# A chunked linear attention with a feed-forward layer: the decays of the first 128 tokens spread over rows on TensorE instead of through DRAM, and a new order

## The chip, the cores and the metric

One core of a Trainium2 chip runs the kernel. The time is device microseconds of one execution; lower is better. Matrix products run on TensorE (PE, its weight loads PEld), elementwise work on VectorE (DVE), ScalarE (ACT) and GpSimd (POOL); SyncE (SP) only issues DMAs, as ScalarE does too.

## What is computed

Four batches of 8 heads, 768 tokens, head size 32, state size 16. The attention is a recurrence cut into pieces: within a piece a product of C and B is weighted by ratios of decays and multiplied with x, and a state is carried on. Then each token (256 wide, all heads side by side) goes through a normalization and two weight matrices, with its input added at the end.

```python
def _attn_ref(x, a, B, C):
    log_a = np.log(np.clip(a, 1e-06, 1.0))
    ...
        cum = np.cumsum(la, axis=-1)
        L = np.exp(cum[:, :, :, None] - cum[:, :, None, :]) * causal
        M = np.einsum('bhin,bhjn->bhij', Cc, Bc) * L
        y[:, :, sl] = np.einsum('bhij,bhjd->bhid', M, xc) + y_inter
...
def _moe_ref(x, g_ln, w_ch1, w_ch2):
    xn = (x - mu) / np.sqrt(var + 1e-06) * g_ln
    ch = np.maximum(xn @ w_ch1, 0.0) @ w_ch2
    return (x + ch).astype(np.float32)
```

## The kernel before

The tokens go in six blocks t = 0 to 5 of 128 tokens of all batches and heads; u = 0, 1 is the half of the batches. Every instruction is written out by hand, in one table of steps (`ISSUE`): a step is a name and its block, half or part, and after a colon the engine (v VectorE, p GpSimd, a ScalarE, s SyncE's queue). Each engine runs its steps in the order of the table, and an instruction that waits holds up all behind it on its engine. A DMA is a step too: it waits on the engine whose queue issues it, and each also waits until the DMA eight places before it in the whole program has landed, since eight semaphores are used in turn.

Steps of the start: `ld:s a` loads the decays with one row for each batch part and head (128 rows of 192), `clip`, `u` and `d` (lines 289 to 298) scan them into products since and until the borders of 32 tokens, `uds`. These stand on 128 rows of 6 x 32, but C and B stand on rows of (head, state) with 512 columns of (batch, token), so each head's decays are wanted on 16 rows. `ro` (line 301) writes `uds` to a DRAM tile `scr`, and `ld ud` (line 134) reads it back with a broadcast over the 16 rows. `C` (line 305) multiplies C by it into `cs`, `B` (line 319) B into `bs`, and `cm` parts `cs` into even and odd heads. `G` (line 345) is the product of the two, `R` (line 351) weights it with `WW`. `WW` is a causal mask (`ones`) overwritten by ratios of decays (`W`), which come from logarithms (`l2` to `l4`), products (`e`) and exponentials (`x`). `V` (line 376) multiplies R by x, `Z` the state's increment (from `be`, B with its decay), `I` adds what the state gives, `y` copies the sum out of PSUM, `yh` and `yl` split it in an upper and a lower part, `T` turns it to tokens and `tc` copies that.

The two weight matrices come as 64-bit integers (`ld w1`, `ld w2`, 512 KB each part) and are turned to floats by `k0` and `kr` (ScalarE, lines 182 and 201), `k1` to `k3` (VectorE) and `f` (GpSimd, line 206); w1 is centred by two float32 products `wc` on TensorE (lines 217, 218); `wh` and `wl` split the result. `h` (line 457) is the first layer for 128 of 1024 hidden columns, in block 0 for each half u by itself, `hh` and `hl` its ReLU split in two; `o` (line 477) is the second layer for one batch, `oe` its end and `od` its store. `fill` is a product of zeros that nothing reads.

PSUM has two pools, one of five banks for the attention and one of three for the rest. `ud`, `c`, `b`, `bt` and `xt` tiles have two buffers each.

Of the kernel before, what the change touches and what calls it, by code (L numbers as in the profile page):

```python
# [50 lines left out]
def shape_constants():  # L51

    k = np.arange(P)
    sub = k // SUB
# [19 lines left out]
def linear_attention_ffn(ctx, tc, xv, a, bt, bn, cn, w1, w2, consts, out):  # L74
    nc = tc.nc
# [33 lines left out]
    scr = dr.tile([2, NT, P, SUB], F32, name="scr")  # L109
# [11 lines left out]
    def load(what, *at, e=nc.sync):  # L121
# [5 lines left out]
        elif what == "ud":  # L127
# [5 lines left out]
            rows = scr[i, t].rearrange("(h c) k -> h (c k)", h=NH)  # L133
# [166 lines left out]
    def spread_out(i, e=nc.sync):  # L300
        e.dma_start(scr[i].rearrange("t r k -> r t k"), uds[:, i].rearrange("p (t k) -> p t k", k=SUB))
# [184 lines left out]
    def fill(i, bank):  # L486
# [106 lines left out]
```

## Time and profile before

| | us |
|---|---|
| median of 3 runs | 211.73 |
| lowest, highest | 209.41, 485.84 |
| the profiled execution | 210.03 |
| its span, first to last instruction | 208.2 |
| TensorE busy in it | 199.8 (96%) |
| VectorE, ScalarE, GpSimd busy | 122.8, 83.1, 54.8 |

The span is what the trace shows; 1.83 us of the execution lie around it. A busy TensorE is not a TensorE at its peak: a product that waits in its pipeline counts as busy.

### The profile page before, as it was taken

The page shows a single profiled execution, that of the slowest core. Times are in us where ns is not written, and L with a number is a line of the kernel's source. Part 1 is how long each engine was busy: PE and PEld are TensorE (multiplying, and loading weights), DVE is VectorE, ACT ScalarE, POOL GpSimd, SP SyncE. Part 2 cuts the span into 40 slices and gives each one's busy share as a digit, 9 for nine tenths or more (in the row PEclk, how much of TensorE's full clock was granted, in tenths as well). Part 3 has the DMA queues.
Part 4 walks back from the last instruction along what each step waited for, and adds up shares of the span by engine and source line. Part 5 has one row for each costly group of instructions (what it writes and reads, how often), then busy time and mean ns, then how long its engine had stood idle before and what let it go on. Part 6 is the DMA issues. An engine that isn't in the chain of part 4 may idle for free.

```text
span 208.2 us, 4661 instructions
## 1 busy us (share of the span) xinstructions
PE 199.8 (96%) x1956; PEld 172.2 (83%) x1956; DVE 122.8 (59%) x258; ACT 83.1 (40%) x170; POOL 54.8 (26%) x57
## 2 busy tenths in 40 slices
PE   8959998999999999999999999999999999999994
PEld 8956466899899876799978899878899889998993
DVE  4847859899958699831657561557443444335310
ACT  3748449889171372431024760143401261123200
POOL 0024533668688065160001821040020000000000
PEclk9996699999999999999999999999999999999999
DMA  6799996073134030012262101010000200001011
GB/s 217 222 296 408 279 254 211 20 238 118 55 127 130 25 122 6 3 17 87 66 212 79 54 0 52 2 50 0 5 3 7 94 0 28 25 0 52 3 50 50
DMA packets 11573, 19.08 MB, mean 92 GB/s; under 512 B 2592, under 2 KB 6048, under 8 KB 11552
## 3 DMA queue, kind: packets, MB, share of 16 engines
q1 hardware_dynamic: 8792, 14.00, 20.9%
q10 hardware_dynamic: 2760, 4.79, 6.9%
q8 instruction: 15, 0.25, 0.5%
q14 instruction: 6, 0.05, 0.1%
HBM read 15.44 MB, written 3.34 MB: 90 GB/s over the span
## 4 chain that ended last, share of the span: by engine, by line
PE 74%; DMA 16%; DVE 5%; issue 2%; SPq 1%; ACT 1%; DVEq 0%
PE po L477 32%; PE ph L457 28%; DMA raw<-in_w_dram 8%; PE G L345 5%; DMA ud<-scr 5%; PE yps L376 4%; PE yt L425 2%; PE yps L364 2%; DMA scr<-uds 2%; DMA a<-in_a_dram 1%; DVE WW L158 1%; DVE hl L469 1%; SPq L134 1%; PE Z L385 1%; DVE R L351 1%
## 5 line engine op out<-in xcount | busy, mean ns | idle before, releaser
L477 PE MATMUL po<-w,hh 128*128 128x256 f32 x384 | 68.7, 281 | 0.0
L477 PEld LDWEIGHTS po<-w,hh 128*128 128x128 f32 x384 | 59.0, 188 | 1.9 <-issue 0.9
L463 ACT ACTIVATE hh<-ph 128x512 fp32r<-128x512 f32 (+1 forms) x56 | 29.7, 541 | 73.7 <-PE ph L457 53.9
L457 PE MATMUL ph<-yh,w 128*128 128x512 f32 (+1 forms) x224 | 55.3, 369 | 1.0 <-DVE hl L469 0.7
L477 PE MATMUL po<-w,hl 128*128 128x256 f32 x192 | 53.6, 279 | 0.0
L469 DVE SCALAR_TENSOR_TENSOR hl<-ph,hh 128x512 fp32r<-128x512 f32 (+1 forms) x56 | 33.7, 607 | 22.8 <-ACT hh L463 22.7
L457 PEld LDWEIGHTS ph<-yh,w 128*128 128x128 f32 x224 | 37.4, 188 | 9.4 <-DVE hl L469 1.8
L351 DVE TENSOR_TENSOR R<-G,WW 128x512 f32<-128x512 f32 x48 | 30.9, 677 | 9.9 <-PE G L345 8.9
L477 PEld LDWEIGHTS po<-w,hl 128*128 128x128 f32 x192 | 36.1, 188 | 0.0
L481 DVE SCALAR_TENSOR_TENSOR o<-po,rstd,ytok 128x256 f32<-128x256 f32 x24 | 11.6, 482 | 34.6 <-PE po L477 34.6
L457 PE MATMUL ph<-yl,w 128*128 128x512 f32 (+1 forms) x112 | 31.3, 360 | 0.5 <-DVE yl L418 0.5
L457 PEld LDWEIGHTS ph<-yl,w 128*128 128x128 f32 x112 | 20.0, 189 | 4.0 <-DVE yl L418 0.7
L345 PE MATMUL G<-cm,bs 32*128 32x256 f32 x192 | 17.3, 421 | 2.6 <-DVE cm L315 2.3
L418 POOL TENSOR_TENSOR yl<-y,yh 128x512 fp32r<-128x512 f32 x8 | 10.2, 1285 | 34.3 <-ACT yh L158 19.7
L345 PEld LDWEIGHTS G<-cm,bs 32*128 32x128 f32 x192 | 10.9, 192 | 6.3 <-issue 3.9
L158 ACT COPY WW<-wt 32x512 f32<-32x512 f32 (+2 forms) x27 | 14.8, 611 | 2.8 <-DVE R L351 2.8
L206 POOL TENSOR_TENSOR top<-top,raw 128x512 int32<-128x512 int32 x8 | 12.0, 1509 | 10.3 <-DVE top L196 4.1
L305 POOL TENSOR_TENSOR cs<-c,ud 128x512 f32<-128x512 f32 x5 | 6.6, 1324 | 26.5 <-DVE c L323 23.4
L376 PE MATMUL yps<-R,xt 128*32 128x128 f32 x384 | 12.1, 274 | 0.0
L376 PEld LDWEIGHTS yps<-R,xt 128*32 128x32 f32 x384 | 10.1, 110 | 1.6 <-DVE top L187 0.8
L490 PE MATMUL idle<-const-float32-0.0 128*128 128x128 f32 x62 | 10.3, 343 | 0.8 <-PEq L581 0.8
L490 PEld LDWEIGHTS idle<-const-float32-0.0 128*128 128x128 f32 x62 | 10.0, 257 | 0.7 <-issue 0.7
(83 smaller groups left out, 179.7 us busy)
## 6 DMA issues: line engine op xcount, KB each, us to landing
out_dram<-o SPq DMA_DIRECT2D x24, 128.0 KB, 1.7
raw<-in_w_dram SPq DMA_DIRECT2D x5, 512.0 KB, 7.4
xt<-in_x_dram SPq DMA_DIRECT2D x5, 512.0 KB, 6.7
ud<-scr SPq DMA_DIRECT2D x7, 256.0 KB
raw<-in_w_dram ACTq DMA_DIRECT2D x3, 512.0 KB, 8.3
b<-in_bn_dram SPq DMA_DIRECT2D x5, 256.0 KB
ud<-scr ACTq DMA_DIRECT2D x5, 256.0 KB
c<-in_cn_dram SPq DMA_DIRECT2D x4, 256.0 KB, 10.0
```

Of the source, the lines that this page charges most:

```text
L158: (e.copy if e is nc.scalar else e.tensor_copy)(dst, src)
L206: e.tensor_tensor(out=f, in0=f, in1=words.pop((w, *at))[0], op=ALU.add)
L345: nc.tensor.matmul(G[q][:, v], bs[r, tok], cm[r, :, tok], start=True, stop=True)
L351: nc.vector.tensor_tensor(out=R.rearrange("p v i k -> p v (i k)"), in0=tiles.pop(("G", t, u, q)).rearrange("p v i k -> p v (i k)"), in1=WW ...
L376: nc.tensor.matmul(tiles["y", t, u, g][32 * k:32 * k + 32, v], x[:, b * NH + h], tiles["R", t, u, h // 2][:, v, h % 2], start=(t == 0), st ...
L418: e.tensor_tensor(out=tiles["yl", t][:, :, tok], in0=tiles["y32", t][:, :, tok], in1=tiles["yh", t][:, :, tok].bitcast(F32), op=ALU.subtract)
L457: nc.tensor.matmul(ph, W1[m // 4, k][:, s, mc], v[:, k, tok], start=(i == 0), stop=(i == len(cmb) - 1))
L463: nc.scalar.activation(tiles["hh", t, m][:, tok], tiles["ph", t, m, u], AF.Relu)
L469: nc.vector.scalar_tensor_tensor(out=tiles["hl", t, m][:, tok], in0=tiles.pop(("ph", t, m, u)), scalar=0.0, in1=tiles["hh", t, m][:, tok]. ...
L477: nc.tensor.matmul(po, tiles[v, t, m][:, cols], W2[m // 2,][:, s, (m % 2) * DM:(m % 2 + 1) * DM], start=(n == 0), stop=(n == len(cmb) - 1))
L481: nc.vector.scalar_tensor_tensor(out=o, in0=tiles.pop(("po", t, b)), scalar=tiles["rstd", t][:, b], in1=tiles["ytok", t][:, b], op0=ALU.mu ...
L490: nc.tensor.matmul(ps.tile([P, P], F32, tag=bank, name=f"idle{i}"), zero.to_broadcast([P, P]), zero.to_broadcast([P, P]), start=True, stop ...
```

## The change

The scan products of block 0 no longer go through `scr`, which now holds five blocks. `U` multiplies the block's 32 columns, repeated 16 times, with a 0/1 matrix that keeps on each row only its own place, and `ur` multiplies the result by a second 0/1 matrix, which sums over rows; the sum of one number and zeros stands in a PSUM bank, in the place of the `ud` tile of block 0. The two matrices make the first load of constants 144 columns wider.

```diff
+C_ROW = C_SUM + 8
+C_COL = C_ROW + P
+C_CAUSAL = C_COL + P // NH
...
+    c[:, C_ROW:C_COL] = (k // DS)[:, None] == (k // DS)[None, :]
+    c[:, C_COL:C_CAUSAL] = (k % (P // NH))[:, None] == np.arange(P // NH)
...
-    scr = dr.tile([2, NT, P, SUB], F32, name="scr")
+    scr = dr.tile([2, NT - 1, P, SUB], F32, name="scr")
...
-            rows = scr[i, t].rearrange("(h c) k -> h (c k)", h=NH)
+            rows = scr[i, t - 1].rearrange("(h c) k -> h (c k)", h=NH)
...
-        e.dma_start(scr[i].rearrange("t r k -> r t k"), uds[:, i].rearrange("p (t k) -> p t k", k=SUB))
+        e.dma_start(scr[i].rearrange("t r k -> r t k"), uds[:, i, SUB:].rearrange("p (t k) -> p t k", k=SUB))
+
+    def own_columns(i, e=nc.vector):
+        m = tiles["m", i] = hp.tile([P, P // NH, SUB], F32, tag="hl", name=f"own{i}")
+        e.tensor_tensor(out=m, in0=uds[:, i, :SUB].unsqueeze(1).to_broadcast([P, P // NH, SUB]), in1=cst[:, C_COL:C_CAUSAL].unsqueeze(2).to_broadcast([P, P // NH, SUB]), op=ALU.mult)
+
+    def all_rows(i):
+        ps = tiles["ud"[i], 0] = ps_att.tile([P, TB], F32, tag="att", name=f"rows{i}")
+        nc.tensor.matmul(ps, cst[:, C_ROW:C_COL], tiles.pop(("m", i)).rearrange("p j k -> p (j k)"), start=True, stop=True)
...
-ld:s a, inv:v, ld:a early, az:p, ini:v, ld:a w1 0 1, clip, ld:a w1 0 0, cf, u, ro:a 0, iv, d, l1, ones:v 0, l2, l3, ro:s 1, l4, k0 1 0 1, fill 0 att,
+ld:s a, ini:v, az:p, clip, inv:v, u, ld:a early, ld:a c 0, iv, ld:s w1 0 0, U:v 0, cf, d, l1, U:v 1, fill 0 att, fill 1 att, fill 2 att, fill 3 att,
```

Of the DMAs, ScalarE's queue keeps the constants and c of block 0; all others are issued by SyncE. There are 25 fills instead of 31. The rest of the table is in another order, with some steps on other engines: over the whole program VectorE gets 17 more instructions (three more `W` copies, three more `yl`, two `U` among them, and three `be` fewer), GpSimd eleven fewer.

VectorE at the start, where block 0's `cs` and `bs` are made; before:

```order
L289 TENSOR_SCALAR AZ<-a_104 128x6x31
L292 SCALAR_TENSOR_TENSOR uds<-AZ,ini 128x192
L295 RECIPROCAL inv<-uds 128x6
L298 SCALAR_TENSOR_TENSOR uds<-AZ,inv 128x192
L244 TENSOR_SCALAR cst<-cst 128x192
L158 COPY WW_91<-cst 128x2048
L253 TENSOR_TENSOR ll<-cst,lh 128x192
L158 COPY WW_92<-cst 128x2048
```

And now, to the same place and on to `bs`:

```order
L299 RECIPROCAL inv<-uds 128x6
L310 TENSOR_TENSOR own_119<-uds,cst 128x512
L302 SCALAR_TENSOR_TENSOR uds<-AZ,inv 128x192
L248 TENSOR_SCALAR cst<-cst 128x192
L310 TENSOR_TENSOR own_124<-uds,cst 128x512
L162 COPY WW_91<-cst 128x2048
L319 TENSOR_TENSOR cs_173<-c_114,rows_160 128x512
L257 TENSOR_TENSOR ll<-cst,lh 128x192
L191 TENSOR_SCALAR top_175<-top_175 128x512
L191 TENSOR_SCALAR top_187<-top_187 128x512
L333 TENSOR_TENSOR bs_201<-b_168,rows_170 128x512
```

The two `own` products come in between the scans, one of the two mask copies (`WW_92`) has gone to ScalarE, and `cs` and `bs` read PSUM (`rows`) and stand ahead of most of the first weights' work (`top`).

ScalarE in the middle of the start, from the first centred weights to the copies of y; before:

```order
L158 CAST w_328<-wc_309 128x512
L182 ACTIVATE top_342<-raw_230 128x512
L182 ACTIVATE top_344<-raw_306 128x512
L152 DMA raw_385<-in_w_dram 128x1024
L158 CAST w_389<-wc_323 128x512
L201 ACTIVATE raw_230<-raw_230 128x512
L158 COPY y_393<-yps_347 128x256
L158 COPY y_393<-yps_367 128x256
```

And now:

```order
L205 ACTIVATE raw_237<-raw_237 128x512
L287 COPY em<-emps 128x96
L288 COPY emt<-emps 128x24
L162 CAST w_319<-wc_308 128x512
L186 ACTIVATE top_324<-raw_279 128x512
L162 CAST w_326<-wc_321 128x512
L186 ACTIVATE top_334<-raw_212 128x512
L162 COPY y_403<-yps_359 128x256
```

The issue of a load of w2 (`raw_385`, part 3) between the casts is gone from ScalarE; `top_324` is the first work on part 0 of w2 (`raw_279`), which SyncE now loads.

SyncE's first loads; before:

```order
L126 DMA a_104<-in_a_dram 128x192
L301 DMA scr<-uds 128x6x32
L142 DMA c_179<-in_cn_dram 128x512
L142 DMA b_194<-in_bn_dram 128x512
L134 DMA ud_203<-scr 128x1x512 x2
L155 DMA cst<-in_consts_dram 128x326
L147 DMA raw_211<-in_w_dram 128x1024
```

And now:

```order
L130 DMA a_104<-in_a_dram 128x192
L151 DMA raw_117<-in_w_dram 128x1024
L151 DMA raw_162<-in_w_dram 128x1024
L146 DMA bt_165<-in_bt_dram 128x512
L146 DMA b_168<-in_bn_dram 128x512
L159 DMA cst<-in_consts_dram 128x326
L151 DMA raw_209<-in_w_dram 128x1024
L156 DMA raw_212<-in_w_dram 128x1024
L151 DMA raw_237<-in_w_dram 128x1024
L146 DMA c_239<-in_cn_dram 128x512
L146 DMA xt_261<-in_x_dram 128x1024
L305 DMA scr<-uds 128x5x32
```

The first two parts of w1 (`raw_117`, `raw_162`) come from SyncE now, and `scr` is written after x of block 0 is issued; part 0 of w2 is the next row.

## Rows read from the trace of the kernel before

**Rows 1.** The top of the page: busy us of each engine, its share of the span of 208.2 us, instructions.

```profile
PE 199.8 (96%) x1956; PEld 172.2 (83%) x1956; DVE 122.8 (59%) x258; ACT 83.1 (40%) x170; POOL 54.8 (26%) x57
```

**Rows 2.** The chain of work that ended last, in order of time: start us, us, what; from 16 us on, and of TensorE's dense part a few pieces of each kind.

```profile
26.26 11.28 DMA raw<-in_w_dram
...
39.55 3.15 PE ph L457 x24
...
51.80 1.08 PE G L345 x16
...
56.91 1.88 PE yps L376 x64
58.80 0.45 PE Z L385 x32
...
84.00 0.44 PE yt L425 x4
...
87.18 1.03 PE yps L364 x32
...
121.37 5.61 PE po L477 x48
...
187.12 6.83 PE ph L457 x30
...
205.19 0.48 DVE o L481
```

**Rows 3.** Instructions in order of time, from 0 to 17 us: start us, us, engine, line, what, count, and in brackets the engine's idle time before it and what ended it.

```profile
0.76 7.43 PE L490 MATMUL idle<-const-float32-0.0 128*128 128x128 f32 x38 [0.76 <-PEq L581]
3.81 0.62 ACT L241 CAST cfr<-cst 128x512 fp32r<-128x512 uint8 x1 [1.81 <-DMA cst<-in_consts_dram]
5.14 1.22 DVE L158 COPY WW<-cst 128x2048 f32<-128x2048 f32 x1
10.03 1.64 ACT L158 COPY WW<-wt 32x512 f32<-32x512 f32 x3
11.48 0.69 DVE L305 TENSOR_TENSOR cs<-c,ud 128x512 f32<-128x512 f32 x1 [1.54 <-DMA ud<-scr]
14.89 1.15 PE L345 MATMUL G<-cm,bs 32*128 32x256 f32 x16 [2.33 <-DVE cm L315]
16.15 1.89 DVE L351 TENSOR_TENSOR R<-G,WW 128x512 f32<-128x512 f32 x3 [0.62 <-PE G L345]
```

**Rows 4.** The same view from 20 to 52 us.

```profile
20.09 2.08 PE L217 MATMUL wc<-top,gd 128*128 128x512 f32 x2
28.30 0.35 ACTq L152 DMA_DIRECT2D raw<-in_w_dram  x1
28.69 0.59 ACT L158 CAST w<-wc 128x512 fp32r<-128x512 f32 x1 [3.00 <-DMA xt<-in_x_dram]
28.95 1.02 PE L218 MATMUL wc<-top,gneg 128*128 128x512 f32 x2
31.47 1.76 DVE L418 TENSOR_TENSOR yl<-y,yh 128x512 fp32r<-128x512 f32 x2 [0.54 <-ACT yh L158]
33.29 0.51 PE L457 MATMUL ph<-yl,w 128*128 128x256 f32 x2 [0.54 <-DVE yl L418]
48.84 0.40 PE L477 MATMUL po<-w,hh 128*128 128x256 f32 x2
```

**Rows 5.** Groups of instructions with their shapes kept apart: line, engine, operation, shapes, count, busy us, mean ns of one, idle us before them.

```profile
L158 ACT COPY y<-yps 128x256 f32<-128x256 f32 x16 | 5.6, 378 | 4.1 <-PE yps L376 3.9
L313 ACT ACTIVATE cm<-cs,cst 128x512 f32<-128x512 f32 x6 | 4.4, 734 | 3.3 <-POOL cs L305 2.8 <-DVE cs L305 0.5
L351 DVE TENSOR_TENSOR R<-G,WW 128x512 f32<-128x512 f32 x48 | 30.9, 677 | 9.9 <-PE G L345 8.9 <-ACT WW L158 1.1
L196 DVE SCALAR_TENSOR_TENSOR top<-raw,top 128x512 int32<-128x512 int32 x8 | 5.3, 681 | 0.0
L191 DVE TENSOR_SCALAR top<-top 128x512 int32<-128x512 int32 x8 | 3.3, 437 | 0.0
L315 POOL TENSOR_SCALAR cm<-cs,cst 128x512 f32<-128x512 f32 x3 | 4.9, 1625 | 0.1
```

**Rows 6.** VectorE's `be` beside a GpSimd instruction and the same operation with GpSimd idle, from the instructions in order of time.

```profile
54.82 1.57 POOL L315 TENSOR_SCALAR cm<-cs,cst 128x512 f32<-128x512 f32 x1
55.08 0.98 DVE L329 TENSOR_TENSOR be<-bt,pend 128x512 f32<-128x512 f32 x1
...
72.08 0.66 DVE L329 TENSOR_TENSOR be<-bt,pend 128x512 f32<-128x512 f32 x1
```

**Rows 7.** Stretches of the span: us, then busy us (instructions) of each engine, TensorE's granted clock, share of the DMA engines, GB/s moved.

```profile
0.00:5.00 5.00, 4.24 (x20) 4.28 (x21) 1.98 (x8) 1.90 (x2) 0.33 (x6) 1.00 0.63 212
5.00:10.00 5.00, 4.92 (x43) 4.73 (x43) 4.79 (x10) 3.53 (x9) 0.00 (x0) 1.00 0.80 227
10.00:15.00 5.00, 2.67 (x27) 2.50 (x27) 2.04 (x5) 2.93 (x7) 0.50 (x2) 1.00 0.86 273
15.00:20.00 5.00, 4.75 (x34) 3.25 (x34) 3.86 (x9) 3.64 (x10) 2.95 (x2) 0.72 1.03 409
20.00:25.00 5.00, 5.00 (x8) 2.23 (x8) 4.18 (x7) 2.61 (x5) 2.86 (x2) 0.60 1.05 308
...
8.00:12.00 4.00, 3.92 (x43) 3.73 (x42) 2.46 (x6) 3.23 (x8) 0.00 (x0) 1.00 0.58 182
```

More of the change, by code (lines that the diff above doesn't have):

```diff
@@ L494, in linear_attention_ffn @@
         ld=load, fill=fill, az=restart, ini=initial, inv=cleared, ones=masks, gm=centring,
-        clip=clipped, u=since, iv=last, d=till, ro=spread_out, C=scaled_c, cm=parted, B=scaled_b, c2=inter, be=ended,
+        clip=clipped, u=since, iv=last, d=till, ro=spread_out, U=own_columns, ur=all_rows, C=scaled_c, cm=parted, B=scaled_b, c2=inter, be=ended,
         cf=exact_cf, l1=clipped_a, l2=logs, l3=logs_h, l4=logs_l, e=sums_to, x=decays_to, so=sums_of, sm=decays_of, mb=apart, sp=spread, em=spread_copy,
@@ new lines @@
+fill 4 att, fill 5 att, fill 6 att, fill 7 att, fill 8 att, fill 9 att, fill 10 att, fill 11 att, fill 12 att, fill 13 att, fill 14 att, fill 15 att,
+fill 16 att, ur 0, ld:s w1 0 1, ones:a 1, ld:s bt 0, l2, ld:s b 0, ur 1, ones:v 0, C:v 0, k0 1 0 0, l3, so, l4, k1 1 0 0, k0 1 0 1, e 3, sm, k1 1 0 1,
+cm:a 0 1, x 3, e 1, ld:s late, B:v 0, e 2, cm:p 0 0, k2 1 0 0, k2 1 0 1, ld:s w1 1 1, mb:v, ld:s w2 2, x 1, fill 17 att, fill 18 att, fill 19 att, G 0
+1, sp, k3 1 0 0, x 2, ld:s w1 1 0, ld:s c 1, W:a 0 1, k3 1 0 1, gm:p, kr 1 0 0, kr 1 0 1, R 0 1 2, e 0, gd 1, f:p 1 0 0, R 0 1 0, R 0 1 1, k0 1 1 1,
@@ new lines @@
+ld:s x 0, ro:s 0, f:p 1 0 1, R 0 1 3, x 0, k0 1 1 0, gd 0, W:a 0 0, k1 1 1 0, k1 1 1 1, kr 2 2, k2 1 1 0, kr 1 1 1, ld:s w2 0, fill 20 att, fill 21
+att, fill 22 att, fill 23 att, G 0 0, ld:s ud 1 0, k2 1 1 1, k3 1 1 0, kr 1 1 0, fill 24 att, wc 0 0, ro:s 1, k3 1 1 1, em, R 0 0 0, R 0 0 3, wh:a 1 0
+0, wc 0 1, k0 2 0, wh:a 1 0 1, ld:s w2 3, be:p 0, ld:s w2 1, k0 2 2, R 0 0 1, f:p 1 1 1, R 0 0 2, Z 0, V 0 0, wl:v 1 0 0, V 0 1, f:p 1 1 0, ld:s ud 1
+1, wl:v 1 0 1, wc 1 0, k1 2 2, k1 2 0, y:a 0 0 1, k2 2 2, k2 2 0, y:a 0 0 0, y:a 0 1 0, ld:s b 3, wc 1 1, ld:s c 3, C:v 1, k3 2 0, kr 2 0, yh:a 0 0,
@@ new lines @@
+1, h 2 5, oe 1 0, h 2 1, yh:v 3 0, cm:v 4 0, od 0 1, T 3 0, hh 2 5, st 2 2, oe 1 1, tc 2 0, c2 4, hh 2 1, h 2 0, hl 2 5, tc 3 0, hh 2 0, hl 2 1, od 1
+1, G 4 1, K:p 4, R 4 1 0, h 2 3, h 2 7, hh 2 3, hl 2 0, h 2 6, st 2 3, sb:p 3, R 4 1 2, R 4 1 1, ld:s ud 5 1, st 2 1, yh:p 3 1, R 4 1 3, hl 2 3, ag 2
+1, ag 2 3, hh 2 7, hl 2 7, G 4 0, yl:v 3 0, ag 2 2, T 3 1, R 4 0 3, h 2 4, od 1 0, R 4 0 2, h 2 2, R 4 0 1, R 4 0 0, I 4, V 4 0, C:p 5, st 3 1, tc 3
+1, hh 2 6, hh 2 4, st 3 3, V 4 1, W:a 5 0, st 2 0, B:v 5, yl:p 3 1, hh 2 2, Z 4, y:a 4 0 1, ag 2 0, hl 2 6, h 3 2, rs 2, od 1 2, y:v 4 1 0, hl 2 2,
@@ new lines @@
+cm:a 5 0, hh 3 2, y:v 4 1 1, S 4, hl 2 4, hl 3 2, o 2 1, o 2 2, y:v 4 0 0, yh:p 4 0, o 2 0, rc 2, W:a 5 1, oe 2 1, cm:a 5 1, T 4 1, oe 2 0, st 3 0, h
+3 7, G 5 1, oe 2 2, ag 3 3, c2 5, R 5 1 3, yh:a 4 1, o 2 3, hh 3 7, h 3 0, od 2 1, R 5 1 2, oe 2 3, hl 3 7, T 4 0, hh 3 0, hl 3 0, ag 3 0, ag 3 1,
+yl:v 4 1, sb:v 4, h 3 4, h 3 3, st 3 2, tc 4 1, yl:p 4 0, R 5 1 0, ld:s x 5, h 3 6, hh 3 4, ag 3 2, hh 3 3, R 5 1 1, rs 3, G 5 0, hh 3 6, hl 3 4, hl 3
+3, h 3 1, hl 3 6, st 4 2, R 5 0 1, R 5 0 2, h 3 5, R 5 0 0, hh 3 1, tc 4 0, R 5 0 3, I 5, st 4 0, od 2 2, V 5 0, hh 3 5, rc 3, V 5 1, y:a 5 0 0, ag 4
@@ L551 @@
+6, od 3 2, hh 5 6, hl 5 2, oe 4 2, h 5 0, od 4 3, hl 5 6, h 5 4, hh 5 0, ag 5 0, od 4 0, od 4 2, h 5 3, ag 5 1, hl 5 0, ag 5 2, h 5 5, hh 5 4, rs 5,
+hh 5 3, hl 5 4, hl 5 3, hh 5 5, hl 5 5, h 5 7, hh 5 7, hl 5 7, rc 5, o 5 1, o 5 2, oe 5 1, oe 5 2, o 5 3, od 5 1, od 5 2, oe 5 3, od 5 3, o 5 0, oe 5
+0, od 5 0
 """
```

60 lines of the change are left out of this document (20 added, 40 removed).

## The prediction

> **What bounds the kernel now.** I read the page's head first: TensorE is busy for 199.8 of 208.2 us, so the question is which of that is work that must be done, and when it can begin [rows 1]. The chain of waits answers it [rows 2]. Up to 39.55 us it goes through loads and other engines; from there it runs mostly through TensorE. Its pieces give a price for each product when they stand close: 24 half-width `h` products 3.15 us, so 0.79 for a half step; five `h` steps 6.83, 1.37 each; two `o` steps 5.61, 2.80 each; `G` 1.08; two `V` 1.88; `I` 1.03; `T` 0.44; `Z` 0.45. After 39.55 us there remain 11 half `h`, 40 `h`, 24 `o`, 10 `G`, 10 `V`, 5 `I`, 10 `T` and 3 `Z`: 8.7 + 54.8 + 67.2 + 10.8 + 9.4 + 5.2 + 4.4 + 1.4 = 161.9 us. The last `o` ends at 205.19, which is 165.6 us later. So only 3.7 us are lost behind 39.55 us, and the kernel's time is the time at which TensorE gets its first hidden-layer work, plus a sum of products that the change leaves alone. The change can win in the start, and only there by much.
>
> The start, in order of time: the first `cs` begins at 11.48 us, held by `ud` coming back from DRAM, `G` at 14.89, the first `R` at 16.15 [rows 3]. The cast of the second half of the weights, ahead of the copies of y on ScalarE, stands still for 3.00 us; just before it is the issue at 28.30 of a load that waited for an earlier load, and the wait is put down to that load [rows 4]. The lower part of y ends at 33.23 (31.47 + 1.76), `h` is complete from then on, and the first `o` starts at 48.84 [rows 4]. That last number is my milestone.
>
> **The change part by part.** Durations are those of the profiled execution, 210.03 us, and the sum is made against it; the median of the three runs, 211.73, is 1.70 above.
>
> *`U` and `ur` for the way through DRAM.* `U` needs the first scan and the first constants, now 301 KB instead of 229 and sharing the DMA engines with w1: they came before 3.81 [rows 3], I take 4.5, by when the scan is done. Neither `U` nor `ur` is in the trace. `U` has 128 x 512 float32 products: 0.69 like `cs` [rows 3], up to 0.98 like `be` beside GpSimd [rows 6]; I take 0.69. The second `U` ends near 7.1 behind the second scan. `ur` is a float32 product with 512 columns: 1.02 at the full clock, 2.08 when the granted clock is at half [rows 4]; I take 1.02, as the clock was at full until 15 us [rows 7]. It stands behind 17 fills: 19 took 7.43 us [rows 3], so 17 end near 7.3, and the two `ur` at 8.3 and 9.4. VectorE meanwhile copies a mask (1.22 [rows 3]) until 8.3. `cs` runs 8.3 to 9.0 instead of 11.48 to 12.17: 3.2 us won. `bs` needs the second `ur` and stands behind `ll` and two `k1`: near 10.9. With one part of `cm` on GpSimd (1.6, so 10.6 [rows 5]), `G` starts near 11 instead of 14.89.
>
> *What is late next: `W`.* ScalarE's chain is mask copy, logarithm, two `k0`, then `cm`, three exponentials, three `W` copies. It waits for `msps` behind the second `ur` (9.8), then 0.73 + 1.15 + 1.64 [rows 3, 5]: 13.4. The mask copy that went to ScalarE is not in the trace there: 1.22 as on VectorE, or four times a 512-column copy of 0.55, 2.2 [rows 3]; either ends before 9.8, so it costs nothing. `R` starts at 13.4 instead of 16.15: only 2.75 of the 3.9 us of `G` are left.
>
> *To the hidden layer.* VectorE: four `R` (2.7) to 16.1; `k0` of the last w1 part ends on ScalarE at 16.9; six weight steps (two of 0.42, two of 0.44, two of 0.68 [rows 5]) to 20.0; four `R` to 22.7; then `wl`, `k1`, `k2`, `cs`, `k3` and the two `yl` (1.76) to 29.6. ScalarE from 13.4 has 18 instructions, at 0.59 each, the middle of 0.38 to 0.73 and a little more [rows 5], 10.6 us without a wait to 24.0, where the y copies begin; the stall of 3.00 us has no counterpart, as that load is issued by SyncE. TensorE: the first pair of `wc` (four products) waits for GpSimd's two `f` and starts near 17.2; at the full clock it ends at 21.3. `V` comes behind the `R`, 22.7 to 24.6, then the second pair of `wc` to 28.7, `T`, and `h` from 29.1. But before, the granted clock was 0.72 and 0.60 from 15 to 25 us [rows 7], at half for much of it, behind a stretch in which TensorE had little to do: it waited 2.33 us for the first `G` [rows 3]. The new order has such a stretch at 14 to 17 us. If all four products of the first pair run at half, they end at 25.5, `V` follows, and `h` starts near 31.9. So 29.1 to 31.9, against 33.23.
>
> *To the first output.* Between the two TensorE has 16 half `h` (12.6), two `G` (2.2) and a `T`: 15.2 us, so 44.3 to 47.1. ScalarE has 15 short `hh` and 25 others of 0.38 to 0.73, about 0.58 each [rows 5]: 5.9 + 14.5 = 20.4 from 24.0, so 44.4 without any wait. VectorE needs 12.5 us of work from 29.6 on: 42.1. So 44.4 at best and 47.1 with the slow clock. I take 45.1, a quarter of the way, since the poor stretch now holds a `G`, two products `e` and five fills and is the shorter one. Against 48.84 that is 3.74 won. TensorE has by then done a `G` more (1.08) and a `Z` fewer (0.45) than before at this point: 0.63 more.
>
> *From there on* the products are the same. VectorE's 17 extra instructions lie beside a TensorE that is dense from 80 us on, with VectorE far from full over the span (59% [rows 1]); I cost them at nothing. If that cover is gone, six `W` copies on VectorE cost up to 6 x 0.7 less the idle time there. The 3.7 us of loss I leave as they are, since the same kind of work meets in the same place.
>
> The sum: 210.03 - 3.74 - 0.63 = 205.66, rounded 205.6.
>
> *A rule against it.* A VectorE `be` took 0.98 us beside a GpSimd `cm`, 0.66 without [rows 6]. The Trainium skill, "SBUF — State Buffer", section "Who interferes with whom", says that the two share a port pair and that the one which starts first keeps it for its whole instruction while the other stands still. The trace agrees in direction. By the rule the new `cm` of block 0 on GpSimd at 9.0 us could hold VectorE's `k1` steps until 10.6, some 1.2 us, and by the `be` rows 0.3; the sum would be 206.8 and 205.9.
>
> **The rivals.**
>
> *More than the start (201.9).* The new order also closes the 3.7 us that TensorE loses behind 39.55 us. For it: VectorE has less to do before the eight `hl` of block 1 are out, since three `be` go to GpSimd. Against it: VectorE is nearly full until 80 us. 205.6 - 3.7 = 201.9.
>
> *The gain melts (209.8).* The start is earlier, but TensorE, VectorE and ScalarE all come to within 1 us of each other at 45 us, and each wait of one is passed to the others. At the half clock for the second pair of `wc` too, four products cost 1.06 us more each, 4.2, and next to nothing is left: 205.6 + 4.2 = 209.8; half of such losses leaves 207 to 208.
>
> *Slower: ScalarE waits for part 0 of w2.* Its first step on it stands, at 22.1 us, ahead of the second w1 cast and the copies of y. SyncE alone now issues all loads ahead of it, in order: 5248 KB with the constants and c, 5.37 MB. By the rates of before (212, 227, 273, 409 GB/s in stretches of 5 us) that much had moved at 19.5 us [rows 7], so it is hidden. From 267 GB/s down, counted from 2 us, it lands after 22.1 and each us is lost. At 212 GB/s it lands at 27.3: 5.2 lost, 210.8. At 182, which the trace shows from 8 to 12 us [rows 7], at 31.5: 9.4 lost, 215.0. For it: eight DMAs in flight at most, each new one behind a landing, on one queue. Against it: in that slow stretch SyncE was waiting for `scr`, which is gone. The Trainium skill, "DMA: Bandwidth & Descriptors", section "Issuing engines are not separate DMA queues", says that all issuers use the same 16 DMA engines, which takes this rival's chance down further; no run here shows it.
>
> **How the numbers follow.** Forecast 0.55, with its own range 203.5 to 207.8: the first `o` at 47.1 gives 207.7, a fast one and some of the lost 3.7 us the lower end; more than the start 0.15; the gain melts 0.18; slower 0.12, of which part ends near 211. Two percent of 210.03 is 4.2 us, about what a measurement can tell from no change. Faster by more needs under 205.8: 0.15 and somewhat over half of the forecast, with the melted case's lower edge, 0.50. Slower by more than 2% is over 214.2; with orders that go wrong in ways not listed, 0.10. The rest, 0.40. The range takes in the better case down to 201.5, and the melted one and the milder half of the slower one up to 210.8.
>
> **What would show it.** `cs` of block 0 near 8.3 us and `G` near 11; the first `R` behind a `W` copy, near 13.4; no ScalarE wait of 3 us ahead of the y copies; the first `h` between 29 and 30.5 and the first `o` near 45; TensorE dense from there, with the last `o` near 200.8. The forecast is wrong if the first `o` comes after 47 us, if ScalarE waits for a load near 22 us, or if TensorE's gaps behind 45 us differ from 3.7 by more than 3 us.

## The result, and the profile after

| | before | after |
|---|---|---|
| median, us | 211.05 | 200.97 |
| ratio, 95% interval | | 0.9544 (0.9469 to 0.9618) |
| the profiled execution, us | 210.03 | 200.64 |
| its span, us | 208.2 | 198.9 |
| lower part of y enters the first `h` step | 33.29 | 26.98 |
| first `o` starts | 48.84 | 40.98 |
| last `o`'s end on VectorE starts | 205.19 | 195.51 |

The changed kernel is 4.6% faster, about 9.6 us; the ratio leaves out one run of the kernel before that took 485.84 us, which the median counts. The prediction said faster, at 205.6 us; 200.97 lies just below its range, which ended at 201.5, and the gain is a little over twice what was forecast. Of the 9.4 us between the two profiled executions, 7.86 are there when the first `o` starts (48.84 - 40.98). A second measurement beside other kernels gave 0.9538 (0.9503 to 0.9573).

The busy line of the page after, to be read against [rows 1]:

```profile
PE 193.7 (97%) x1948; PEld 167.8 (84%) x1948; DVE 127.2 (64%) x275; ACT 82.2 (41%) x166; POOL 48.2 (24%) x46
```

TensorE has 6.1 us less busy time for nearly the same work. The largest pieces are the 192 matmuls of `G` (17.3 us before, 13.9 now), `wc` (10.4 and 8.3, as it now runs at the full clock throughout) and the fills (10.3 and 8.8); the two `ur` add 1.9. The chain of waits after, start us, us, what:

```profile
0.76 6.00 PE idle L504 x34
6.75 1.72 PE rows L315 x4
...
12.09 1.13 ACT raw L205 x2
...
14.95 1.81 DVE top L191 x2
...
18.63 1.81 DVE R L365 x3
...
20.48 2.12 PE yps L390 x60
...
26.67 6.57 PE ph L471 x54
```

No DMA is left in it. Before, the same stretch ran through the load at 26.26 of [rows 2] and, ahead of it, through these two:

```profile
9.84 6.39 DMA raw<-in_w_dram
...
16.25 10.00 DMA ud<-scr
```

Now it is engines all the way, and 54 half-width matmuls, nine half `h` steps, follow each other from 26.67 us.

After, in order of time, 0 to 17 us, beside [rows 3] (start us, us, engine, line, what, count, idle before and what ended it):

```profile
6.59 1.88 PE L315 MATMUL rows<-own,cst 128*128 128x512 f32 x4
7.65 0.69 DVE L319 TENSOR_TENSOR cs<-c,rows 128x512 f32<-128x512 f32 x1
8.44 1.86 POOL L329 TENSOR_SCALAR cm<-cs,cst 128x512 f32<-128x512 f32 x1 [7.58 <-DVE cs L319]
8.53 1.17 DVE L191 TENSOR_SCALAR top<-top 128x512 f32<-128x512 f32 x2
10.44 1.15 PE L359 MATMUL G<-cm,bs 32*128 32x256 f32 x16
10.46 1.62 ACT L162 COPY WW<-wt 32x512 f32<-32x512 f32 x3
11.99 1.22 ACT L205 ACTIVATE raw<-raw 128x512 int32<-128x512 uint32 x2
12.28 2.47 DVE L365 TENSOR_TENSOR R<-G,WW 128x512 f32<-128x512 f32 x4
14.27 0.65 ACT L186 ACTIVATE top<-raw 128x512 f32<-128x512 f32 x1
14.95 1.81 DVE L191 TENSOR_SCALAR top<-top 128x512 f32<-128x512 f32 x2 [0.20 <-ACT top L186]
15.24 1.24 POOL L343 TENSOR_TENSOR be<-bt,pend 128x512 f32<-128x512 f32 x1
15.59 1.02 PE L221 MATMUL wc<-top,gd 128*128 128x512 f32 x2
```

`cs` starts at 7.65 instead of 11.48 and the first `R` at 12.28 instead of 16.15. (`wc` shows here as two matmuls per product, four products for each half of w1.) What the prediction did not look for: ScalarE takes up the third part of w1 (`raw`) at 11.99, and the first `wc` starts at 15.59 instead of 20.09 [rows 4]. On to 41 us:

```profile
16.45 1.02 PE L222 MATMUL wc<-top,gneg 128*128 128x512 f32 x2
...
18.56 2.47 DVE L365 TENSOR_TENSOR R<-G,WW 128x512 f32<-128x512 f32 x4
...
21.79 0.92 ACT L162 COPY y<-yps 128x256 f32<-128x256 f32 x3 [0.90 <-PE yps L390]
...
26.43 0.72 PE L471 MATMUL ph<-yh,w 128*128 128x256 f32 x4
26.98 0.40 PE L471 MATMUL ph<-yl,w 128*128 128x256 f32 x2
...
40.98 0.50 PE L491 MATMUL po<-w,hh 128*128 128x256 f32 x2
```

The stretches, as in [rows 7] (busy us of each engine, granted clock, DMA share, GB/s), and the stretch from the first `o` to the last:

```profile
5.00:10.00 5.00, 5.00 (x42) 3.74 (x41) 4.97 (x10) 4.23 (x9) 1.56 (x1) 1.00 1.04 407
10.00:15.00 5.00, 4.38 (x49) 3.65 (x47) 4.80 (x11) 5.00 (x13) 3.26 (x4) 1.00 1.06 392
15.00:20.00 5.00, 4.85 (x52) 2.28 (x46) 5.00 (x9) 5.00 (x12) 2.71 (x3) 1.00 0.76 251
20.00:25.00 5.00, 4.71 (x70) 2.86 (x67) 5.00 (x11) 4.07 (x10) 1.32 (x2) 1.00 0.84 308
...
40.98:195.51 154.53, 154.49 (x1596) 136.78 (x1592) 90.54 (x198) 47.04 (x91) 29.73 (x27) 1.00 0.16 50
```

From 5 to 15 us the loads move at 407 and 392 GB/s, where [rows 7] have 227 and 273, and the granted clock never leaves the full level, where it was 0.72 and 0.60 from 15 to 25 us.

### The profile page after: what moved, and what is told of

Read it like the earlier page. It is cut to its first block, busy times and chain, and to the rows that moved or that the text cites. A ratio compares the mean times of both kernels' runs of the same rounds, so it can differ in the third digit from the quotient of the medians.

```text
span 198.9 us, 4635 instructions
## 1 busy us (share of the span) xinstructions
PE 193.7 (97%) x1948; PEld 167.8 (84%) x1948; DVE 127.2 (64%) x275; ACT 82.2 (41%) x166; POOL 48.2 (24%) x46
## 4 chain that ended last, share of the span: by engine, by line
PE 92%; ACT 3%; DVE 3%; issue 1%
PE ph L471 34%; PE po L491 34%; PE yps L390 6%; PE G L359 5%; PE idle L504 3%; PE yt L439 3%; PE yps L378 3%; PE wc L221 1%; DVE top L191 1%; DVE R L365 1%; PE Z L399 1%; PE rows L315 1%; PE wc L222 1%; ACT WW L162 1%; ACT raw L205 1%
## 5 line engine op out<-in xcount | busy, mean ns | idle before, releaser
L432 POOL TENSOR_TENSOR yl<-y,yh 128x512 fp32r<-128x512 f32 x5 | 6.9, 1374 | 43.7 <-DVE mv L454 43.5
L210 POOL TENSOR_TENSOR top<-top,raw 128x512 int32<-128x512 int32 x8 | 11.3, 1430 | 12.8 <-ACT raw L205 6.3
L359 PE MATMUL G<-cm,bs 32*128 32x256 f32 x192 | 13.9, 400 | 0.0
L359 PEld LDWEIGHTS G<-cm,bs 32*128 32x128 f32 x192 | 8.9, 184 | 3.1 <-issue 1.8
L162 ACT COPY y<-yps 128x256 f32<-128x256 f32 x14 | 4.9, 378 | 15.2 <-PE yps L390 15.2
L444 ACT COPY ytok<-yt 128x512 f32<-128x512 f32 x12 | 6.8, 584 | 9.0 <-PE yt L439 9.0
L504 PE MATMUL idle<-const-float32-0.0 128*128 128x128 f32 x50 | 8.8, 338 | 1.4 <-PEq L595 0.8
```

Of the source, the lines that this page charges most:

```text
L162: (e.copy if e is nc.scalar else e.tensor_copy)(dst, src)
L210: e.tensor_tensor(out=f, in0=f, in1=words.pop((w, *at))[0], op=ALU.add)
L359: nc.tensor.matmul(G[q][:, v], bs[r, tok], cm[r, :, tok], start=True, stop=True)
L432: e.tensor_tensor(out=tiles["yl", t][:, :, tok], in0=tiles["y32", t][:, :, tok], in1=tiles["yh", t][:, :, tok].bitcast(F32), op=ALU.subtract)
L504: nc.tensor.matmul(ps.tile([P, P], F32, tag=bank, name=f"idle{i}"), zero.to_broadcast([P, P]), zero.to_broadcast([P, P]), start=True, stop ...
```

## The experiments

Two theories stood against each other: that the gain comes down the chain that the prediction followed (`cs`, `G` and `R` of block 0 earlier), and that it comes from the loads, which no longer stand behind the way through DRAM. A third question was which single wait of the old start is worth something. Ratios are to the kernel before on the same chip. Each kernel has a short name, e1 to e17.

**One part alone.** First the products in the old order (e1). `scr` and its writes shrink to five blocks; the writes move behind `ld:s bt 0`, since block 1 is their first reader.

```diff
-u, ro:a 0, iv, d, l1, ... ro:s 1, ... fill 17 att, fill 18 att, ... ld:s ud 0 0, ... ld:s ud 0 1, ... ld:s bt 0,
+u, iv, U:v 0, d, l1, U:v 1, ... ur 0, ur 1, ... ld:s bt 0, ro:s 0, ro:s 1,
```

> The kernel before, in its own order, with block 0's decays by the two products instead of through DRAM, and nothing else. Theory A (the way through DRAM was the price): cs of block 0 comes 1.5 to 3 us earlier, and the first hidden product with it: 207 to 208.5. Theory B (what decides is the order and the waits behind it, above all ScalarE's stall at the issue of part 3 of w2 until x of block 1 has landed): the earlier cs is given back at that stall, 209.5 to 210.5.

205.84 us, 0.9765 (0.9688 to 0.9841), more than either theory gave. Then the new order with the DRAM way put back (e4; `U` and `ur` out, `ro:a 0` behind `cf`, `ro:s 1` and both reads behind `ld:s b 0`):

```diff
-U:v 0, ... U:v 1, ... ur 0, ... ur 1, ... ro:s 0, ... ro:s 1,
+cf, ro:a 0, ... ld:s b 0, ro:s 1, ld:s ud 0 0, ld:s ud 0 1,
```

> The changed kernel in its new order, with the products taken out again: block 0's decays go through DRAM, written by ScalarE and SyncE and read back by SyncE right behind b of block 0, as in the kernel before. Theory A: it loses most of the gain, 207 or more. Theory B: cs comes 3 to 4 us later than with the products, some of it is hidden by the weights' work, and the new order keeps half or more of the gain: 203 to 205.

206.96 us, 0.9845 (0.9743 to 0.9947), nearer to theory A; `cs` at 13.96 us, first `o` at 47.97. The product of the two ratios, 0.961, is near the change's 0.9544, as if each part brought its own gain. The products' is the larger by these numbers, but the two intervals overlap.

**Where the products' gain comes from.** The kernel of e1 again, for its trace (e5):

> The kernel before in its own order with the two products alone, once more, for its trace; its time is known (ratio 0.9765). Theory D (the loads: the start of before ends with the landing of the last part of w2 at 37.5 us, behind everything that SyncE issues later because it stood behind the DRAM way): parts 1 and 3 of w2 are issued some 3 to 5 us earlier than 26.26 and 28.30, and the first o comes by as much as it is faster. Theory A' (only the chain cs, G, R counts): cs, G and R each come 3 us or more earlier and the w2 issues stay within 1 us.

204.91 us. `cs` hardly moved, from 11.48 to 11.02, and the first `R` came 1.9 us earlier (14.22), yet the first `h` matmul starts at 26.43, 5.6 us earlier than in the kernel before:

```profile
32.01 0.74 PE L457 MATMUL ph<-yh,w 128*128 128x256 f32 x4 [0.33 <-ACT yh L158]
```

The chain from `cs` to `R` can have given 1.9 of that at most; the other 3.7 us arise behind the first `R`. Parts 1 and 3 of w2 are issued at 20.42 and 22.39, 5.8 and 5.9 us earlier than before, and the first `o` starts at 43.55, 5.3 us earlier: the chain of waits still goes through part 1, as in [rows 2], but from an earlier issue:

```profile
20.42 11.83 DMA raw<-in_w_dram
```

Its rows, then two stretches of it:

```profile
8.69 2.50 POOL L214 TENSOR_SCALAR gneg<-cst 128x2 f32<-128x2 f32 x1 [7.83 <-DMA cst<-in_consts_dram]
11.02 0.68 DVE L319 TENSOR_TENSOR cs<-c,rows 128x512 f32<-128x512 f32 x1
14.22 1.89 DVE L365 TENSOR_TENSOR R<-G,WW 128x512 f32<-128x512 f32 x3 [0.62 <-PE G L359]
17.21 1.12 PE L221 MATMUL wc<-top,gd 128*128 128x512 f32 x2
26.43 0.71 PE L471 MATMUL ph<-yh,w 128*128 128x256 f32 x4
```

```profile
5.00:10.00 5.00, 4.76 (x40) 3.61 (x38) 5.00 (x10) 3.07 (x8) 1.31 (x1) 1.00 1.04 389
10.00:15.00 5.00, 4.74 (x47) 4.15 (x46) 4.38 (x10) 5.00 (x12) 3.74 (x3) 1.00 1.08 392
```

The loads run at 389 and 392 GB/s. To test it, the products stay, and block 0's way through DRAM goes on as dead traffic at its old places, read into a tile that nothing uses (e9):

```diff
+        elif what == "dead":
+            i, = at
+            rows = scr[i, 0].rearrange("(h c) k -> h (c k)", h=NH)
+            e.dma_start(dead[:, i], rows.unsqueeze(1).to_broadcast([NH, DS, TB]))
...
+u, ro:a 0, iv, U:v 0, ... ro:s 1, ... ur 0, ur 1, ... ld:s dead 0, ... ld:s dead 1,
```

> The kernel before, in its own order, with the products U and ur for block 0, while block 0's way through DRAM is kept as traffic that nothing needs: the writes of the scans for all six blocks at their old places, and the two reads with a broadcast at their old places on SyncE's queue into a tile that no instruction reads. Theory 'loads': the products' own gain (205 us against 211, first h at 26.4 us instead of over 32) comes from SyncE's queue and the DMA engines, which no longer stand behind the write and the two reads of small pieces. With the dead traffic SyncE again waits for the write, the loads behind it come as late as before: w2 part 1 issued near 26 instead of 20.4, first h near 31 to 33, 208.5 to 211 us. Rival 'chain': the gain comes from cs, G and R of block 0 being ready earlier. The products are still there, so the first R stays near 14.2, first h near 26 to 28, 204.5 to 206 us.

212.74 us, 1.0104 (1.0053 to 1.0156): the products' whole gain is gone, and 1% on top. One look at the same kernel, for its trace (e15):

> One look at the kernel with the products and the whole dead way through DRAM, for its trace. Theory 'loads': first R near 14 to 15 us, as with the products alone, but w2 part 1 issued near 26 us and not near 20.4, DMA at 210 to 280 GB/s from 5 to 15 us and not at 390, first h over 31 us.

211.5 us:

```profile
11.07 0.69 DVE L324 TENSOR_TENSOR cs<-c,rows 128x512 f32<-128x512 f32 x1
15.63 0.23 POOL L219 TENSOR_SCALAR gneg<-cst 128x2 f32<-128x2 f32 x1 [14.78 <-DMA cst<-in_consts_dram]
15.64 0.31 DVE L283 TENSOR_TENSOR mblk<-msum,cst 32x120 f32<-32x120 f32 x1 [2.89 <-DMA cst<-in_consts_dram]
16.48 1.87 DVE L370 TENSOR_TENSOR R<-G,WW 128x512 f32<-128x512 f32 x3
16.84 0.67 ACT L210 ACTIVATE raw<-raw 128x512 int32<-128x512 uint32 x1 [2.73 <-DMA raw<-in_w_dram]
20.40 2.07 PE L226 MATMUL wc<-top,gd 128*128 128x512 f32 x2
33.20 0.74 PE L476 MATMUL ph<-yh,w 128*128 128x256 f32 x4 [0.33 <-ACT yh L167]
```

```profile
5.00:10.00 5.00, 5.00 (x26) 3.98 (x25) 5.00 (x10) 2.24 (x5) 0.00 (x0) 1.00 0.82 232
10.00:15.00 5.00, 4.82 (x55) 4.15 (x54) 2.75 (x6) 4.10 (x10) 0.00 (x0) 1.00 0.81 266
```

`cs` is where it was (11.07), but GpSimd waits until 15.63 for the second load of constants and ScalarE until 16.84 for the third part of w1; `wc`, which needs both, starts at 20.40, at the half clock, and `h` at 33.20. The first `R` did not stay near 14, as was expected: VectorE stands 2.89 us for the same constants in an instruction ahead of it (`mblk`), so `R` comes at 16.48. Theory "loads" is shown: with early decays but late loads nothing is won, and the loads hold up `R` too. So "chain" falls in the sense that early decays are not enough; `R` itself was not held early here. Nor was the clock parted from the loads: the first four products of `wc` take 5.5 us here and 3.7 in e5. The kernel before has the same wait for w1:

```profile
16.25 0.68 ACT L201 ACTIVATE raw<-raw 128x512 int32<-128x512 uint32 x1 [2.79 <-DMA raw<-in_w_dram]
```

Two halves of the dead way. The reads without their wait (e13; the source is a part of c's last block), and the wait without the reads' bytes (e14):

```diff
-            rows = scr[i, 0].rearrange("(h c) k -> h (c k)", h=NH)
+            rows = cn[NT - 1][i * NH:(i + 1) * NH]
```

> As the kernel with the products and a dead way through DRAM (212.7 us, against 205 without the dead reads), but the two dead reads, same shape and broadcast and at the same places on SyncE's queue, read a part of c's last block, which is there from the start, so that SyncE doesn't wait for the write of the scans. The dead writes stay. Theory 'wait': what costs is that SyncE stands in front of the two reads until the write has landed, and all loads behind them are issued late. Without the wait the loads are issued as with the products alone: first h at 26.4 to 27.5 us, 204.5 to 206.5 us. Rival 'traffic': the reads themselves take the DMA engines' time away from the loads behind them: first h stays over 30, 209 to 213 us.

```diff
-            e.dma_start(dead[:, i], rows.unsqueeze(1).to_broadcast([NH, DS, TB]))
+            e.dma_start(dead[0:1, i, 0:P], scr[i, 0].rearrange("r k -> (r k)")[0:P].unsqueeze(0))
```

> The other half: the two dead reads wait for the write of the scans, at the same places on SyncE's queue, but read 512 bytes each into one row instead of 2 KB into each of 128 rows. Theory 'wait': as with the whole dead way, first h over 30 us, 209 to 213 us. Rival 'traffic': as with the products alone, 204.5 to 206.5 us.

210.48 us, 0.9994 (0.9961 to 1.0027), and 208.48 us, 0.9902 (0.9858 to 0.9945); first `h` at 31.52 and 28.76. Against the whole dead way at 1.0104, taking the wait away brings 1.1%, taking the reads' bytes away 2.0%; neither theory is the whole, and together they are 3.1 of the 3.4% between e9 and e1. The rest, 0.3%, is within the intervals. So, if the two simply add, which no run tells, little is left for the place of the writes, though at the old place SyncE issues nothing before the scan is done, as its waits in the kernel before show (waited for: us, times, longest):

```profile
SPq L301 <- DVE cst L244: 4.1, 1, 4.1
```

That place was not tried by itself, and within the reads their longer issue on SyncE (1.42 us for both, 0.77 in e14) and their bytes were not parted.

If the loads are all, they could go first without any products. The kernel before, with four loads ahead of SyncE's write (e17):

```diff
-ro:s 1, ... ld:s c 0, ... ld:s b 0, ... ld:s late, ... ld:s w1 1 1,
+ld:s c 0, ld:s b 0, ld:s late, ld:s w1 1 1, ro:s 1,
```

> The kernel before with its way through DRAM, but c, b, the rest of the constants and the third part of w1 are issued ahead of SyncE's write of the scan, which in the kernel before they stand behind (SyncE issues nothing from 1.1 to 5.1 us). Theory 'loads': a part of what the products bring is only that these loads need not stand behind SyncE's waits; w1 arrives earlier and TensorE has wc earlier, but the decays come later from DRAM (cs near 13 instead of 11.5): 207 to 210 us. Rival: nothing is won, since the decays and G come late by as much as the weights come early: 209.5 to 213 us.

211.41 us, 1.0107 (1.0065 to 1.0150): 1% slower. From the trace of an execution of 209.66 us:

```profile
8.50 0.23 POOL L210 TENSOR_SCALAR gneg<-cst 128x2 f32<-128x2 f32 x1 [7.65 <-DMA cst<-in_consts_dram]
14.06 0.69 DVE L305 TENSOR_TENSOR cs<-c,ud 128x512 f32<-128x512 f32 x1 [3.18 <-DMA ud<-scr]
16.90 1.15 PE L345 MATMUL G<-cm,bs 32*128 32x256 f32 x16 [4.08 <-DVE cm L315]
22.10 2.08 PE L217 MATMUL wc<-top,gd 128*128 128x512 f32 x2
```

The constants are there at 8.50, but now the decays are late: TensorE stands 4.08 us before `G`, and as each engine works in order, `wc` behind it starts at 22.10, at the half clock. In this execution `h` (32.08) and the first `o` (48.43) come about when they did before; where the 1% is lost the trace does not show. The start has two gates, decays and weights. Either one early and the other late gives 1.01 (e9, e17), and in both runs the late one came later than in the kernel before (`cs` at 14.06 here, w1 at 16.84 in e15); both early gives 0.9765. The way through DRAM forced a choice, and the products end it.

**Single waits of the old start.** The load of w2 that ScalarE issued goes to SyncE (e2):

```diff
-V 0 1, ld:a w2 3, k2 2 0,
+V 0 1, ld:s w2 3, k2 2 0,
```

> The kernel before with one step moved: part 3 of w2 is issued by SyncE instead of ScalarE, at the same place in the table. Theory B: the stall of 3.0 us on ScalarE goes, the y copies and the first hidden product come 2 to 2.6 us earlier: about 208. Theory A: ScalarE then waits for the products behind it instead, at most 1 us is won: 209 to 210.

211.02 us, 0.9969 (0.9921 to 1.0017). The issue is gone from ScalarE, which then waits 3.88 us for `wc` instead; first `h` at 32.18, first `o` at 49.15. Nine fills more ahead of the first `G` (e3):

```diff
-fill 30 att,
+fill 30 att, fill 31 att, fill 32 att, ... fill 39 att,
```

> The kernel before with nine more fills ahead of the first G, where TensorE stood idle from 12.6 to 14.9 us. Theory C (the clock): the granted clock stays at 1.0 between 17 and 24 us, the two wc take 4.1 instead of 5.6 us, and 1.5 us of the whole are won: about 208.5. Theory B: the clock stays up, but ScalarE stands at its load until 28.3 us all the same: 209.7 to 210.5.

210.23 us, 0.9990 (0.9948 to 1.0031). The first `wc` runs at the full clock (18.93 us, 1.12), and still `h` starts at 31.60 and `o` at 48.87. Two parts of w2 ahead of x (e6):

```diff
-ld:s w2 2, ... ld:a w2 3, ... ld:s w2 1,
+ld:s w2 2, ld:s w2 3, ld:s w2 1,
```

> The kernel before, its DRAM way and its order kept, but parts 3 and 1 of w2 are issued by SyncE right behind part 2, some 13 us earlier, ahead of x of block 0. Theory D: ScalarE no longer waits for w2 at 36.7 and 37.6 us; x of block 0 lands later in exchange: 207.5 to 209.5. Theory A': nothing is won, 210 or more, up to 213 since x is later.

209.28 us, 0.9960 (0.9923 to 0.9996); 0.4% is won, barely clear of the interval; x of block 0 comes later for it, and TensorE waits 1.15 us for it at `V`. Removed singly, each wait is followed by another. The same move in the kernel of e1 (e10):

```diff
-ld:s w2 2, k2 1 1 0, ... ld:a w2 3, ... ld:s w2 1,
+ld:s w2 2, ld:s w2 3, ld:s w2 1, k2 1 1 0,
```

> The products U and ur in the old order, and parts 3 and 1 of w2 issued by SyncE right behind part 2 (in the old order part 3 was issued by ScalarE in the middle of the start and part 1 by SyncE some 20 us in). With the products alone the first h is at 26.43 us, as early as in the changed kernel, but the first o at 43.55 instead of 40.98, and w2's wait stands in the chain. Theory 'w2': the 2.6 us between are ScalarE's waits for w2 parts 3 and 1; they go, first o near 41, 203 to 203.8 us. Rival 'order': the 2.6 us come from the order in which ScalarE and VectorE do hh, hl and the weight steps; first o stays near 43 to 44, 204.5 to 206 us, or x comes later, as when w2 was loaded early in the kernel before, and the first h with it.

205.08 us, 0.9778 (0.9739 to 0.9817), as with the products alone. From the first `h` to the first `o` it takes 15.4 us instead of 17.1, so theory "w2" is right on that wait; but the first `wc` now ran partly at the half clock and `h` came 1.5 us later, which gives it back (first `o` at 43.28, not near 41).

**The new order's fills.** After without fills 17 to 24, which stand ahead of the two `G` and the first `wc` (e7):

```diff
-fill 17 att, fill 18 att, fill 19 att, G 0 1, ... fill 20 att, ... fill 23 att, G 0 0, ... fill 24 att, wc 0 0,
+G 0 1, ... G 0 0, ... wc 0 0,
```

> The changed kernel without its eight fills 17 to 24, which stand between the exponentials' products and the first wc. Theory C, in the new order: the granted clock falls to half for a stretch, wc takes up to twice its 3.5 us, and 0.7 to 3 us are lost: 201.8 to 204. If the new order itself keeps TensorE busy enough, the clock stays and the time is 200.5 to 201.2.

201.75 us, 0.9611 (0.9548 to 0.9674), with these rows:

```profile
17.20 2.08 PE L221 MATMUL wc<-top,gd 128*128 128x512 f32 x2
...
28.93 0.72 PE L471 MATMUL ph<-yh,w 128*128 128x256 f32 x4
```

Without them the clock does fall to half, for the first `G` (2.09 us instead of 1.15) and the first two products of `wc`, and `h` is 2.5 us later; in the ratio 0.7% is left of it, which the intervals don't part. And twelve instead of seventeen fills ahead of `ur` (e8):

```diff
-fill 11 att, fill 12 att, fill 13 att, fill 14 att, fill 15 att, fill 16 att, ur 0,
+fill 11 att, ur 0,
```

> The changed kernel with 12 instead of 17 fills at the start, so that TensorE is free at 5 us, when the first own columns are ready (5.3 us), and not at 6.6. If the fills hold the first product: cs and all behind it come up to 1.3 us earlier, 199.8 to 200.5. If the clock is still at half at 5.3 us, each of the products takes 2 us instead of 0.9 and nothing is won: 200.8 to 202.

200.49 us, 0.9541 (0.9474 to 0.9607); first `h` at 25.89. The full clock holds with fewer.

**GpSimd beside VectorE.** `be` of block 0 moved behind the last of w1's four `f` steps (the expectation calls it the third), `Z` ahead of `T` (e11); then the same with twelve fills (e12):

```diff
-be:p 0, ... f:p 1 1 1, ... Z 0, V 0 0, ... f:p 1 1 0, ... T 0 1,
+f:p 1 1 1, ... V 0 0, ... f:p 1 1 0, be:p 0, ... Z 0, T 0 1,
```

> The changed kernel with GpSimd's be of block 0 moved behind the third f step, and TensorE's Z, which needs it, moved ahead of T. In the changed kernel the first two k1 steps of the next w1 part on VectorE take 1.81 us each beside this be, against 0.76 for a pair elsewhere. Theory 'port': the two slow each other, so VectorE saves about 1 us there, wc follows earlier, first h 25.4 to 26.0 instead of 26.43, 199.8 to 200.5 us. Rival 'hidden': VectorE's time there is covered by wc on TensorE; first h unchanged, 200.6 to 201.2 us.

> The same with 12 instead of 17 fills ahead of the two ur. With 12 fills alone the changed kernel measured 200.5 us, first h 25.89. Theory 'port': both gains add, first h near 25, 199.3 to 200.0 us. Rival 'hidden': as with twelve fills alone, 200.3 to 200.8 us.

200.72 us, 0.9559 (0.9530 to 0.9587), and 200.01 us, 0.9530 (0.9505 to 0.9556). The changed kernel, beside e13 and e14 (e16):

> The changed kernel itself, on one chip with the others and against the kernel before, for a narrower ratio to set beside the versions with be later (0.9559) and be later with twelve first fills (0.9530): 200.6 to 201.2 us, 0.954 to 0.959; if the twelve fills and the later be gain anything it lies above 0.9556.

200.38 us, 0.9538 (0.9503 to 0.9573). In e11 the pair of `k1` at 14.65 takes 0.88 instead of 1.81 (both together, not each as the expectation has it), the second half of `wc` starts 1.14 us earlier (21.39 against 22.53) and `h` only 0.4 earlier (26.02), as y's lower part and the weights' casts follow at their own pace. The time of e11 lies in the range of "hidden", that of e12 between the two. No version is shown to beat the changed kernel; twelve fills with the later `be` may be 0.4 us better, which these intervals don't tell.

## Why the prediction was wrong

The direction, the place of the gain (the start) and the order of events held. The sizes did not: the term "to the hidden layer" was too long by 2.67 us, the clock's by 0.7, "to the first output" by 0.75, and 1.19 us more were won behind it. The reason given for the gain, earlier decays, was half of the cause; the loads are the other half.

*What bounds the kernel.* Right that TensorE is dense behind 39.55 us and that the start decides. But the chain of waits had said what the start waited for, a load issued at 26.26 and under way for 11.28 us [rows 2], and the text passed over it with "loads and other engines". It then followed the engines only, `cs` to `G` to `R`.

*`U` and `ur`.* `cs` was put at 8.3 and `G` at 11, measured 7.65 and 10.44. The two `ur` took 1.88 together, priced at 2.04, and 17 fills ended at 6.76, not 7.3. The first `R` began at 12.28 instead of 13.4, but not behind a `W` copy: those had ended at 12.08, and VectorE, which had no idle time before it, was just ending its `k3`.

*"To the hidden layer"*, the first step that failed. By it `k0` ends on ScalarE at 16.9, the second `R` begin at 20.0, y is copied from 24.0 and `h` starts at 29.1 at best; measured 14.92, 18.56, 21.79 and 26.43. What was mis-sized is ScalarE's work: its `W` ended at 12.08 instead of 13.4, and the six instructions from there to the end of `k0` took 0.47 us each, where 0.59 was priced; that makes the 1.98 at `k0`. VectorE's six weight steps gave 0.54 of it back (3.64 instead of 3.1): its two `k1` beside `be` took 1.81, priced at 0.84, and the other four less than priced. So 1.44 are left ahead of the second `R`. Of the other 1.23, 0.23 lie in the `R` themselves and the rest in `V`, `wc` and `T`: products of `wc` start 0.86 us apart when they stand close (15.59 and 16.45), and were priced at 1.02 each. None of it waited for a load. The prediction let ScalarE run without waits but never asked whether the weights would be there; in the old order, e15 shows that with the loads as before they are not, and `h` starts at 33.20.

*The clock.* It was given 0.7 us (45.1 instead of 44.4), with up to 2.8 as the bad end. There was no dip; e7 shows that the eight later fills are the reason, and that 2.5 us at `h` would have been the price.

*"To the first output."* 15.3 us from `h` to `o`, measured 14.55: 0.75 less. A half `h` step was priced at 0.79 from [rows 2]; standing close it took 0.73 (nine in 6.57), which over 16 of them is about the difference.

These three terms are the whole miss at the milestone: 2.67 + 0.7 + 0.75 = 4.12 us, 45.1 against 40.98.

*"From there on."* The losses behind the first `o` were left as they are. From first to last `o` it was 156.35 us and is 154.53; 0.63 of that was foreseen, so 1.19 us of waiting went. TensorE's idle time in that stretch fell only from 0.35 to 0.04 us; the rest is waiting inside products that count as busy, above all in `G`, whose matmuls there took 70 ns each instead of 78 (9.24 us for 132, 11.19 for 144). What comes behind the last `o` and around the span is 0.29 longer. 4.12 + 1.19 - 0.29 = 5.02, from 205.66 to 200.64.

*The rivals.* "More than the start" came nearest in number (201.9), by luck: only 1.2 of its 3.7 us came about, and the rest of the extra gain was in the start. "The gain melts" needed the half clock twice. "Slower" needed under 267 GB/s for part 0 of w2; the loads moved at about 400, and ScalarE worked on it at 19.15 us without a wait. The prediction had the reason in hand there ("in that slow stretch SyncE was waiting for `scr`, which is gone"), used it to take a chance from a rival, and did not turn it into a gain. The Trainium skill, "DMA: Bandwidth & Descriptors", section "Issuing engines are not separate DMA queues", was cited there too. Now a run agrees: with nearly all loads issued by SyncE alone, the 16 DMA engines were full from 5 to 10 us (share 1.04, 407 GB/s).

*The rule on the port.* VectorE's two `k1` beside `cm` took 1.17, a pair at 22.15 us with GpSimd idle 0.74: 0.4 lost, near the 0.3 by the `be` rows [rows 6], not the 1.2. Beside `be` a pair took 1.81. The Trainium skill, "SBUF — State Buffer", section "Who interferes with whom", fits the second: the first `k1` runs free, the other stands until `be` ends at 16.48, and 0.37 more gives 16.85; it ended at 16.76. By it the pair beside `cm` would have ended past 10.3; it ended at 9.70. There the measurement decides against the rule, and who pays is not fixed either: in e7, e8, e11 and e12 the same pair beside the same `cm` took 0.75 to 0.76, and `cm` 2.57 instead of 1.86, so that `G` waited for `cm` (0.91 us in e8).

## What to carry to other kernels

When the chain of waits at the start is made of DMA pieces, ask what the queue that issues them stands behind: a round trip through DRAM costs not only its consumer, but every load queued behind its waits and its bytes. A start with two gates, here decays and weights, gained nothing when one was opened at the other's expense, and a single wait removed was followed by the next. So a wait that is worth nothing when it is removed alone need not be harmless. A reason that lowers a rival's chance is to be followed to the end: if a resource is freed, say what else becomes early.

## What the runs showed that was not expected

- The small pieces of the scans' write do not hold the DMA rate down by themselves: in e5 they are issued from 4.63 us on, beside loads that move at 389 GB/s from 5 to 10 us. In e15, where the rest of the constants and w1 are issued only from 9.53 us on, the rate is 232.
- Two reads of 256 KB that nothing uses cost 2.0% of the kernel (e9 against e14), as they stand ahead of the loads that open the start.
